# Head-major loads and quadrant transposes for part of q and k in a fused attention and feed-forward kernel

## The chip, the cores and the metric

The kernel runs on one core of one Trainium2 chip. The metric is the device time of one execution in microseconds (us), lower is better. A kernel is executed several times in alternation with the kernel before on the same chip; executions are marked fast or slow by time and by TensorE's granted clock, and only fast ones are compared. Profiles are of single executions; their span starts at the first instruction and is about 2 us shorter than the device time.

Names: PE is TensorE's matmul, PEld its weight load, DVE VectorE, ACT ScalarE, POOL GpSimd, SP SyncE. L907 is line 907 of the kernel whose profile is shown.

## The reference

Sliding-window causal attention with a linear bias, followed by a gated feed-forward over the 8 heads joined. B is 8, H 8, S 576, D 64, and everything comes and goes in float32.

```python
scores = q @ k.T / sqrt(D)                       # per batch and head
mask = (rel >= 0) & (rel < 128)                  # rel = query position - key position
scores = where(mask, scores - slope[h] * abs(rel), -1e9)
attn = softmax(scores)
x = (attn @ v) joined over heads                 # [8, 576, 512]
x_prev = x shifted by one position
xk = mu_k * x + (1 - mu_k) * x_prev              # xr in the same way
k = relu(xk @ w_k); v = (k * k) @ w_v            # 512 -> 1024 -> 512
out = sigmoid(xr @ w_r) * v
```

## The kernel before

The kernel is written as a graph of operations with durations and priorities. When it is built, a small simulator inside it (`plan`) picks, engine by engine, the ready operation of best priority, and the instructions are emitted in that order. So the order on each engine is fixed in the program, and every change of a load, a duration or a setting lets the simulator pick a new order for all engines.

Scores need q and k with the head dimension on the partitions. They are loaded with the positions on the partitions, cast to bf16 by the DMA, and transposed by PE against an identity. Two heads of 64 make one 128x128 transpose, so the two heads must lie side by side for a fixed row `r`, and each (position, head) is a run of its own: 64 float32, 256 bytes. The code is cut and shortened.

```python
def half_load(i, part, r, h0, h1):               # batch 0, second half (part 1)
    src = (q, k)[i][0, h0:h1, 256 * part:256 * part + 256].rearrange("h (p r) d -> p h r d", p=128)
    dst = half_buf[:, part, i, r, h0:h1]         # [p, part, i, r, h, d]: heads adjacent for one r
    return dma(POOL, ..., lambda e: nc.gpsimd.dma_start(out=dst, in_=src[:, :, r]))

def full_load(b, i, h, g):                       # a whole later batch: four DMAs, one per r
    src = (q, k)[i][b, :, 0:SM].rearrange("h (p r) d -> p h r d", p=128)   # (XB batches: cut)
    return [dma(POOL, ..., lambda e, r=r: nc.gpsimd.dma_start(
        out=cb_buf[h.idx][:, i, r], in_=src[:, :, r]), [g]) for r in range(NF)]

def qk_full(b, g, prio):                         # two heads: 8 transposes, 1 bank, 1 copy on ACT
    hp, hq = Hold(PT), Hold("qk")
    def emit_t(e):
        for n in range(2 * NF):
            nc.tensor.transpose(one(hp).bitcast(BF16)[:, 128 * n:128 * n + 128],
                cb_buf[hc.idx][:, n // NF, n % NF, 2 * g:2 * g + 2].rearrange("p h d -> p (h d)"), ident)
    t = op(PE, 0.0565 * 8, cl[b] + paced(b, g), prio + (3,), emit_t, [hp, hq], [hc])
    y = op(ACT, act_t(1024), [t], prio + (3,), lambda e: copy_any(e, ...), (), [hp])
# ... batch 0, part 1 does the same with half_buf and four transposes a pair of heads ...

LOADS = 'vK23tVkabcRWw'   # order of loads: K, k = halves of w_k, 2 = q and 3 = k of part 1,
                          # t = last 64 positions of batch 0, a b c = batch 1, R W w = other weights
MMASK = True              # the decay mask made by PE (mask_pe) and one exp; False: by ACT from dist
NWARM = 90                # matmuls of zeros, lowest priority: they fill PE where nothing is ready
for i in range(NWARM):
    plan.add(PE, 0.118 if i < 40 else 0.056, 0.0, [n_warm, g_wm], (1e12, i), emit_warm, (), [h_wm])
```

The softmax here doesn't subtract the row's maximum and nothing guards it: scores larger than these inputs give would overflow.

## Time and profile before

| | before |
|---|---|
| device time, three first runs | 237.60, 237.68, 238.79 us |
| span of the profiled run | 235.8 us, clock 1.00 |
| busy share PE / DVE / ACT / POOL | 96 / 80 / 68 / 43% |
| DMA packets under 512 bytes | 129,304 of 138,555 |

PE is the bound. The windows view gives, for each stretch, the busy time of PE, PEld, DVE, ACT and POOL with the number of instructions, then the granted clock, DMA share and GB/s. Kernel before:

```profile
core 0: us, PE busy (x) PEld busy (x) DVE busy (x) ACT busy (x) POOL busy (x), PEclk, DMA share, GB/s
20.00:25.00 5.00, 5.00 (x82) 3.13 (x81) 2.26 (x8) 4.46 (x10) 4.08 (x6) 1.00 2.27 162
25.00:30.00 5.00, 4.51 (x65) 3.61 (x62) 4.96 (x16) 4.08 (x10) 4.70 (x6) 1.00 2.41 151
```

Between 20 and 25 us PE counts as full while DVE is idle more than half of the time: a stage with room. Between 25 and 30 DVE is full and PE is not.

### The profile page before, as it was taken

The page shows a single profiled execution, that of the slowest core. Times are in us where ns is not written, and L with a number is a line of the kernel's source. Part 1 is how long each engine was busy: PE and PEld are TensorE (multiplying, and loading weights), DVE is VectorE, ACT ScalarE, POOL GpSimd, SP SyncE. Part 2 cuts the span into 40 slices and gives each one's busy share as a digit, 9 for nine tenths or more (in the row PEclk, how much of TensorE's full clock was granted, in tenths as well). Part 3 has the DMA queues.
Part 4 walks back from the last instruction along what each step waited for, and adds up shares of the span by engine and source line. Part 5 has one row for each costly group of instructions (what it writes and reads, how often), then busy time and mean ns, then how long its engine had stood idle before and what let it go on. Part 6 is the DMA issues. An engine that isn't in the chain of part 4 may idle for free.

```text
span 235.8 us, 5966 instructions
## 1 busy us (share of the span) xinstructions
PE 227.3 (96%) x2334; PEld 138.7 (59%) x2363; DVE 188.5 (80%) x425; ACT 160.5 (68%) x280; POOL 102.3 (43%) x128
## 2 busy tenths in 40 slices
PE   7999989999999999999999999999999999999993
PEld 7586776557575765555565765455665754445462
DVE  7393976999787999999998999974789995984242
ACT  3749799659988978984986684938475826326260
POOL 8878885697886595197109646100000000000000
PEclk9999999999999999999999999999999999999999
DMA  6999999999999999999999999995331224121112
GB/s 162 181 146 163 154 145 195 157 203 193 154 131 177 138 138 203 134 125 154 204 159 118 97 190 188 154 103 140 114 78 49 89 70 119 46 92 47 69 64 89
DMA packets 138555, 31.45 MB, mean 133 GB/s; under 512 B 129304, under 2 KB 134944, under 8 KB 138528
## 3 DMA queue, kind: packets, MB, share of 16 engines
q0 software_dynamic: 110992, 16.26, 109.5%
q1 hardware_dynamic: 25792, 14.23, 28.5%
q10 hardware_dynamic: 1744, 0.59, 1.0%
q8 instruction: 18, 0.29, 0.6%
q14 instruction: 9, 0.07, 0.1%
HBM read 33.56 MB, written 9.44 MB: 182 GB/s over the span
## 4 chain that ended last, share of the span: by engine, by line
PE 82%; ACT 7%; DMA 4%; issue 3%; POOL 3%; DVE 0%; DVEq 0%; POOLq 0%
PE uno L929 26%; PE uno L895 23%; PE uno L913 13%; PE duo L704 6%; PE duo L646 6%; DMA qx<-in_k_dram 4%; ACT rl L902 2%; PE uno L759 2%; ACT qk L616 2%; ACT at L660 2%; PE uno L1116 2%; POOL qx L430 1%; PE duo L633 1%; POOL vs L433 1%; PE uno L704 1%
## 5 line engine op out<-in xcount | busy, mean ns | idle before, releaser
L929 PE MATMUL uno<-wv_sb,kk 128*128 128x512 bf16 (+2 forms) x283 | 70.3, 373 | 0.9 <-issue 0.3
L895 PE MATMUL uno<-xk,wk_sb 128*128 128x256 bf16 (+2 forms) x412 | 69.4, 313 | 0.6 <-ACT qk L616 0.3
L660 ACT ACTIVATE at<-duo 128x1024 bf16<-128x1024 f32 (+2 forms) x68 | 65.9, 1008 | 2.7 <-PE duo L646 2.4
L902 ACT ACTIVATE rl<-uno 128x256 bf16<-128x256 f32 (+2 forms) x104 | 47.8, 506 | 19.5 <-PE uno L895 16.0
L895 PEld LDWEIGHTS <-wk_sb 128*128 128x128 bf16 x416 | 38.8, 98 | 22.1 <-issue 1.4
L868 DVE TENSOR_TENSOR kk<-rl 128x256 bf16<-128x256 bf16 (+2 forms) x104 | 33.6, 338 | 15.5 <-ACT rl L902 14.1
L929 PEld LDWEIGHTS <-kk 128*128 128x128 bf16 x296 | 26.5, 98 | 26.4
L433 POOL DMA_DIRECT2D vs<-in_v_dram x32 | 28.3, 897 | 28.2 <-PE duo L704 25.1
L920 ACT ACTIVATE rs<-uno 128x512 bf16<-128x512 f32 x36 | 22.1, 614 | 26.7 <-PE uno L913 24.3
L673 DVE TENSOR_TENSOR at<-at,mask 128x1024 bf16<-128x1024 bf16 x54 | 36.1, 684 | 3.5 <-ACT at L660 3.4
L913 PE MATMUL uno<-wr_sb,xr 128*128 128x512 bf16 x133 | 36.1, 379 | 0.5
L934 DVE SCALAR_TENSOR_TENSOR ot<-rs,uno 128x512 f32<-128x512 bf16 (+2 forms) x37 | 24.5, 667 | 14.5 <-PE uno L929 9.8
L455 POOL DMA_DIRECT2D cb<-in_k_dram x28 | 24.8, 902 | 11.6 <-DMA vs<-in_v_dram 4.9
L616 ACT COPY xt<-uno 128x320 bf16<-128x320 bf16 (+1 forms) x45 | 16.0, 404 | 15.2 <-PE uno L759 12.5
L455 POOL DMA_DIRECT2D cb<-in_q_dram x28 | 24.7, 906 | 2.5 <-DMA vs<-in_v_dram 1.0
L704 PEld LDWEIGHTS <-at 128*128 128x128 bf16 x576 | 21.9, 98 | 6.6 <-issue 1.1
L809 DVE SCALAR_TENSOR_TENSOR xk<-dl,mu_sb,xt 128x576 bf16<-128x576 bf16 (+1 forms) x32 | 24.9, 779 | 0.3
L809 DVE SCALAR_TENSOR_TENSOR xr<-dl,mu_sb,xt 128x576 bf16<-128x576 bf16 (+1 forms) x32 | 24.7, 776 | 0.0
L913 PEld LDWEIGHTS <-xr 128*128 128x128 bf16 x144 | 13.5, 98 | 14.6
L616 ACT COPY qk<-uno 128x1024 bf16<-128x1024 bf16 (+1 forms) x22 | 19.2, 929 | 2.3 <-PE uno L1014 1.9
L704 PE MATMUL duo<-vs,at 128*128 128x65 bf16 x448 | 19.1, 194 | 0.3 <-ACT at L660 0.2
L715 DVE TENSOR_TENSOR xu<-duo,rc 128x640 bf16<-128x640 f32 x20 | 16.4, 819 | 0.2
(73 smaller groups left out, 206.6 us busy)
## 6 DMA issues: line engine op xcount, KB each, us to landing
out_dram<-ot SPq DMA_DIRECT2D x28, 256.0 KB, 4.9
vs<-in_v_dram POOLq DMA_DIRECT2D x32, 128.0 KB, 6.5
cb<-in_q_dram POOLq DMA_DIRECT2D x28, 128.0 KB, 7.6
cb<-in_k_dram POOLq DMA_DIRECT2D x28, 128.0 KB, 7.0
out_dram<-ot SPq DMA_DIRECT2D x14, 128.0 KB, 1.8
wk_sb<-in_moe_w_k_dram POOLq DMA_DIRECT2D x2, 512.0 KB, 7.9
wv_sb<-in_moe_w_v_dram POOLq DMA_DIRECT2D x2, 512.0 KB, 10.7
qx<-in_k_dram ACTq DMA_DIRECT2D x4, 128.0 KB, 4.8
```

The lines of the kernel that those rows point to most:

```text
L433: return dma(POOL, 256, issue_t(1024), lambda e: nc.gpsimd.dma_start(out=vs_buf[h.idx][:, j, :, 0:D], in_=v[b, :, 128 * j:128 * j + 128].r ...
L455: return [dma(POOL, 256, issue_t(1024), lambda e, r=r: nc.gpsimd.dma_start(out=cb_buf[h.idx][:, i, r], in_=src[:, :, r]), [g]) for r in ra ...
L616: (nc.scalar.copy if e == ACT else nc.vector.tensor_copy)(out=out, in_=in_)
L660: lambda e, ah=ah, w=w, hp=hp: nc.scalar.activation(out=ah(), in_=two(hp)[:, :, 0:w], func=AF.Exp, scale=float(scale)), (), [hp])
L673: nc.vector.tensor_tensor(out=a, in0=a, in1=m, op=ALU.mult)
L704: nc.tensor.matmul(a[:, hl, t - t0], lhsT=at[:, lo:lo + 128], rhs=vs[:, u, 2 * g + hl, :] if u < NF else tvb[:, 2 * g + hl], start=(u == u ...
L809: lambda e: nc.vector.scalar_tensor_tensor(out=buf[hk.idx][:, g, e0 + c0:e0 + c1], in0=dls(), scalar=mu[:, g:g + 1], in1=xc(1), op0=ALU.mu ...
L868: nc.vector.tensor_tensor(out=out, in0=in_, in1=in_, op=ALU.mult)
L895: nc.tensor.matmul(one(hp)[:, 0:n], lhsT=wk_sb[:, po, 128 * fo:128 * fo + 128], rhs=xk_buf[hx.idx][:, po, c0:c1], start=(po == 0), stop=(p ...
L902: a = op(ACT, act_t(n), [s], pr, lambda e, hp=hp, hr=hr: nc.scalar.activation(out=rl_buf[hr.idx][:, 0:n], in_=one(hp)[:, 0:n], func=AF.Rel ...
L913: nc.tensor.matmul(one(hp), lhsT=xr_buf[hx.idx][:, po, 128 * c:128 * c + 128], rhs=wr_sb[:, po], start=(po == 0), stop=(po == NPO - 1))
L929: nc.tensor.matmul(one(hv)[:, a:b], lhsT=kk_buf[hk.idx][:, fo, o:o + 128], rhs=wv_sb[:, fo, a:b], start=(fo == 0), stop=(fo == NFO - 1))
```

## The change

The intent is to have the second half of batch 0's q and k earlier, and batch 1's cheaper, by longer runs. In head-major order a (position group, head) pair is one run of two rows (512 bytes) for batch 0 and four rows (1024 bytes) for batch 1. The price is the layout: for a fixed row the two heads are no longer side by side, so the kernel no longer takes both in one transpose. Each 128x128 block becomes four 64x64 transposes, one in each quadrant of the array; the two row halves write to two PSUM banks, and each bank has a copy of its own. The four part-1 loads also move ahead of the first half of w_k, and ten settings of the scheduler were tuned with the rest.

```diff
-    LOADS = 'vK23tVkabcRWw'
-    XD = 7
+    LOADS = 'v23KtVkabcRWw'
+    XD = 6
-    WAIT = 0.0
+    WAIT = 2.0                                   # price of a change between PE modes in the plan
-    XT0 = (ACT, DVE)
-    QK0 = (ACT,)
+    XT0 = (ACT,)
+    QK0 = (ACT, DVE)                             # who copies batch 0's q and k
-    XTT = range(8, B)
-    MMASK = True
+    XTT = range(6, B)                            # batches whose tails a DMA transposes
+    MMASK = False
-    A = {PE: 10.00, ACT: 3.00, DVE: 5.00, VIR: 0}
-    NBIAS = 5
-    XRL = 4.0
+    A = {PE: 14.25, ACT: 4.00, DVE: 4.50, VIR: 0}
+    NBIAS = 4                                    # groups whose bias PE adds
+    XRL = 3.0
-    SLOPE = 4.6
+    SLOPE = 4.5
-    def half_load(i, part, r, h0, h1):
...
+    def run_load(dst, i, b, c0, r, h0, h1, deps=()):
+        hs = (q, k)[i][b, h0:h1, c0:c0 + 128 * r].rearrange("h (p r) d -> p h (r d)", p=128)
+        return dma(POOL, RUN[r] * (h1 - h0), issue_t(128 * (h1 - h0)), lambda e: nc.gpsimd.dma_start(
+            out=dst()[:, i, h0:h1].rearrange("p h r d -> p h (r d)"), in_=hs), deps)
...
+    def qk_quad(b, g, nr, buf, deps, prio, c0, hq, take, free):
+        hp = [Hold("p1"), Hold("p1")]
+        def emit(e):
+            for n in range(2 * nr):
+                for hl, r in ((0, 0), (1, 1), (1, 0), (0, 1)):
+                    rows = slice(64 * r, 64 * r + 64)
+                    nc.tensor.transpose(
+                        one(hp[r]).bitcast(BF16)[64 * hl:64 * hl + 64, 64 * n:64 * n + 64],
+                        buf()[rows, n // nr, 2 * g + hl, n % nr], ident[rows, rows])
...  (two copies, one for each bank; batch 1 and part 1 of batch 0 call this; the rest as before)
```

More of the change, by code (lines that the diff above doesn't have):

```diff
@@ L220 @@
     RATE = 284.0
+    WIDE = (1,)
+    PART_WIDE = True
+    QUAD = 0.0565
+    RUN = {2: 64 * 284 / 329.0, NF: 128 * 284 / 357.0}
     FLIP = 1.25
     NO = 5
-    WAIT = 0.0
+    WAIT = 2.0
     QM = 0
@@ L262 @@
         "p (a i r h d) -> p a i r h d", a=2, i=2, r=2, d=D)
+    part_buf = qx_buf[0].rearrange("p i g s -> p (i g s)")[:, 2048:4096].rearrange(
+        "p (i h r d) -> p i h r d", i=2, r=2, d=D)
+    wide_buf = [c.rearrange("p i r h d -> p (i r h d)").rearrange(
+        "p (i h r d) -> p i h r d", i=2, r=NF, d=D) for c in cb_buf]
     stage = qx_buf[1].rearrange("p i g s -> p (i g s)").bitcast(FP32).rearrange(
@@ L422, in issue_t @@
         return 0.53 + 0.00034 * nd
-    def half_load(i, part, r, h0, h1):
-        src = (q, k)[i][0, h0:h1, 256 * part:256 * part + 256].rearrange(
-            "h (p r) d -> p h r d", p=128)
-        dst = half_buf[:, part, i, r, h0:h1]
-        nh = h1 - h0
-        return dma(POOL, 32 * nh, issue_t(128 * nh),
-                   lambda e: nc.gpsimd.dma_start(out=dst, in_=src[:, :, r]))
+    def run_load(dst, i, b, c0, r, h0, h1, deps=()):
+        hs = (q, k)[i][b, h0:h1, c0:c0 + 128 * r].rearrange("h (p r) d -> p h (r d)", p=128)
+        return dma(POOL, RUN[r] * (h1 - h0), issue_t(128 * (h1 - h0)), lambda e: nc.gpsimd.dma_start(
+            out=dst()[:, i, h0:h1].rearrange("p h r d -> p h (r d)"), in_=hs), deps)
     def v_load(b, j, h, deps=()):
@@ L450, in tail_load, with wide_load @@
         return h, ns
+    def wide_load(b, h, g, h0, h1):
+        return [run_load(lambda: wide_buf[h.idx], i, b, 0, NF, h0, h1, [g]) for i in range(2)]
     def full_load(b, i, h, g):
@@ L513 @@
     n_row = [mu_load(0, moe_mu_k), mu_load(1, moe_mu_r)]
-    th, tl, n_w, src1 = {}, {}, {}, []
+    th, tl, n_w, src1 = {}, {}, {}, {}
     vl[0] = []
@@ L529, in load_step @@
         elif what in "23":
-            src1.extend(half_load(int(what) - 2, 1, r, 0, 8) for r in range(2))
+            h0 = 4 * (int(what) - 2)
+            src1[h0 // 4] = [run_load(lambda: part_buf, i, 0, 256, 2, h0, h0 + 4) for i in range(2)]
         elif what == "t":
@@ L543, in load_step @@
             batch_load(1, what)
-    ch, cl, xbh, xbl, tth, ttl, ttg = {}, {}, {}, {}, {}, {}, {}
+    cw, ch, cl, xbh, xbl, tth, ttl, ttg = {}, {}, {}, {}, {}, {}, {}, {}
     def tail_flip(b):
@@ L559, in batch_load @@
             g_ = virtual("cb", [ch[b]])
-            cl[b] = full_load(b, 0, ch[b], g_) + full_load(b, 1, ch[b], g_)
+            if b not in WIDE:
+                cl[b] = full_load(b, 0, ch[b], g_) + full_load(b, 1, ch[b], g_)
+            else:
+                cw[b] = [wide_load(b, ch[b], g_, 4 * j, 4 * j + 4) for j in range(2)]
         elif what == "b":
@@ L980 @@
              (((3, 384, 128), (3, 512, 64), (4, 512, 64)), 512)))
+    def qk_quad(b, g, nr, buf, deps, prio, c0, hq, take, free):
[7 more added lines that the diff above has]
+                        buf()[rows, n // nr, 2 * g + hl, n % nr], ident[rows, rows])
+        t = op(PE, QUAD * 2 * nr, list(deps) + [n_ident], prio + (3,), emit,
+               hp + ([hq] if take else []), free)
+        t.rows, t.lazy = (64, 64), True
+        w = 64 * nr
+        ys = [op(QK0 if b == 0 else ACT, {ACT: act_t(2 * w), DVE: dve_t(2 * w)}, [t], prio + (3,),
+                 lambda e, r=r: copy_any(
+            e, qk_buf[hq.idx][:, :, c0 + w * r:c0 + w * r + w].rearrange("p t (c r) -> p t c r", r=nr),
+            one(hp[r]).bitcast(BF16)[:, 0:2 * w].rearrange("p (t r c) -> p t c r", t=2, r=nr)),
+                 (), [hp[r]]) for r in range(2)]
+        return hq, ys
     xks, xrs = {}, {}
@@ L1002 @@
             else:
-                cs = src1
-            hp = Hold("p1")
+                cs = src1[g // 2]
+            hp = Hold("p1") if part == 0 else None
             def emit_t(e, part=part, g=g, hp=hp, f32=f32):
@@ L1015, in emit_t @@
                             one(hp).bitcast(BF16)[:, 128 * nn:128 * nn + 128],
-                            half_buf[:, part, i, r, 2 * g:2 * g + 2].rearrange("p h d -> p (h d)"),
+                            half_buf[:, 0, i, r, 2 * g:2 * g + 2].rearrange("p h d -> p (h d)"),
                             ident)
-            cold = 1.8 if part == 0 and g < 2 else 1.0
-            t = op(PE, (0.115 if f32 else 0.0565) * 4 * cold, cs + [n_ident], prio + (3,), emit_t,
-                   [hp] + ([hq0[g]] if part == 0 else []))
-            y = op(QK0, {ACT: act_t(512), DVE: dve_t(512)}, [t], prio + (3,),
-                   lambda e, part=part, g=g, hp=hp, f32=f32: copy_any(
-                e, qk_buf[hq0[g].idx][:, :, 0:256],
-                one(hp).rearrange("p (t c) -> p t c", t=2)) if f32 else copy_any(
-                e, qk_buf[hq0[g].idx][:, :, 256 * part:256 * part + 256].rearrange(
-                    "p t (c r) -> p t c r", r=2),
-                one(hp).bitcast(BF16)[:, 0:512].rearrange("p (t r c) -> p t c r", t=2, r=2)),
-                (), [hp])
+            if part:
+                ys = qk_quad(0, g, 2, lambda: part_buf, cs, prio, 256, hq0[g], False, [])[1]
+            else:
+                cold = 1.8 if part == 0 and g < 2 else 1.0
+                t = op(PE, (0.115 if f32 else 0.0565) * 4 * cold, cs + [n_ident], prio + (3,), emit_t,
+                       [hp] + ([hq0[g]] if part == 0 else []))
+                ys = [op(QK0, {ACT: act_t(512), DVE: dve_t(512)}, [t], prio + (3,),
+                       lambda e, part=part, g=g, hp=hp, f32=f32: copy_any(
+                    e, qk_buf[hq0[g].idx][:, :, 0:256],
+                    one(hp).rearrange("p (t c) -> p t c", t=2)) if f32 else copy_any(
+                    e, qk_buf[hq0[g].idx][:, :, 256 * part:256 * part + 256].rearrange(
+                        "p t (c r) -> p t c r", r=2),
+                    one(hp).bitcast(BF16)[:, 0:512].rearrange("p (t r c) -> p t c r", t=2, r=2)),
+                    (), [hp])]
             ha = Hold("at")
@@ L1033 @@
                 s, (x,) = scores(0, g, [(pieces, m0, htt if uses_tt else None)], True, hq0[g], ha,
-                              [y, n_dist] + list(n_copy.values()) + n_sid[2 * g:2 * g + 2] +
+                              ys + [n_dist] + list(n_copy.values()) + n_sid[2 * g:2 * g + 2] +
                               (n_tt if uses_tt else []) + ([s] if j else []), prio,
@@ L1141 @@
                 pace = []
-                if not QM:
+                if b in WIDE:
+                    two_q[:] = [qk_quad(b, g, NF, lambda b=b: wide_buf[ch[b].idx], cw[b][g // 2] + paced(b, g),
+                                        prio, 0, Hold("qk"), True, [ch[b]])]
+                elif not QM:
                     two_q[:] = [qk_full(b, g, prio)]
@@ L1145 @@
                     two_q[:] = qk_some(b, g, QM, prio)
-                hq, y = two_q[g % max(QM, 1)]
+                hq, y = two_q[0 if b in WIDE else g % max(QM, 1)]
             _, (m0, m1) = scores(b, g, [HALF0 + (None,), HALF1 + (htt,)], 4 * b + g < NBIAS, hq, ha,
```

## The prediction

> **What bounds the kernel now.** I read the page's totals first, then the slices, then the chain that ended last and PE's timeline.
>
> ```profile
> PE 227.3 (96%) x2334; PEld 138.7 (59%) x2363; DVE 188.5 (80%) x425; ACT 160.5 (68%) x280; POOL 102.3 (43%) x128
> PE   7999989999999999999999999999999999999993
> PE 82%; ACT 7%; DMA 4%; issue 3%; POOL 3%; DVE 0%; DVEq 0%; POOLq 0%
> ```
>
> PE is busy 96% of the span and nearly full in every slice but the first and last. DVE (80%) and ACT (68%) are not the bound over the whole. So a change pays if it takes work off PE, or fills a gap of PE. But "busy" includes 90 warm matmuls (L607) that compute nothing. The chain and PE's timeline show where they stand:
>
> ```profile
> 2.26 1.87 POOL vs L433 x2
> 4.13 0.76 POOL wk_sb L465
> 4.88 2.58 POOL qx L430 x3
> 7.47 8.53 DMA qx<-in_k_dram
> 16.04 0.90 PE uno L1014 x13
> ...
> 30.39 1.25 ACT qk L616 x2
> ...
> 32.06 1.07 ACT qk L616
> ...
> 33.41 0.91 ACT qk L616
> ```
> ```profile
> 12.48 1.56 PE L607 MATMUL uno<-warm 128*128 128x128 bf16 x25
> ...
> 13.98 1.17 PE L607 MATMUL uno<-warm 128*128 128x128 bf16 x18
> ...
> 16.04 0.90 PE L1014 MATMUL uno<-ident,qx 128*128 128x128 bf16 x13 [0.38 <-DMA qx<-in_k_dram]
> ...
> 29.27 0.61 PE L1116 MATMUL uno<-ident,cb 128*128 128x128 bf16 x8
> ```
>
> The end hangs first on the issue of four loads, then on the landing of the second half of batch 0's k at 16.0; until then PE spins on warm matmuls. Around 30 to 34 us the chain runs through ACT's copies of batch 1's q and k out of PSUM; from 38 us it is almost only PE.
>
> **A ledger of PE.** I priced every PE instruction after 9.18 us (the first attention product with v) from the chain's rows: 512 columns 0.216 us (L929 x4, 0.86), 256 columns 0.109 (L895 x8, 0.87), 65 columns 0.030 (L704 x18, 0.55), a 128x128 transpose 0.056 (L1116 x16, 0.89), work on 64 rows half of that, as two run side by side. A change between 128-row and 64-row work costs about 0.08: in
>
> ```profile
> 45.84 0.86 PE uno L913 x4
> 46.70 0.55 PE duo L646 x12
> 47.25 0.97 PE uno L929 x4
> ```
>
> the twelve score matmuls are 8 x 0.055 + 4 x 0.015 = 0.50, and together the middle and last rows are 0.16 above price, for two changes. Walking the built program with these prices gives 215.7 us from 9.18 to the last matmul; the trace needs 222.7 (its last PE piece ends at 231.9). So 7 us are lost to waits and bubbles. Set against the timeline, 3.4 us of it is lost before 32.3 (0.6 at the first v, 0.7 around the landing at 16, 1.6 between 27 and 32 where xu on DVE and the qk copies on ACT are late), 1.7 up to 69 and some 2 in crumbs later. About 3.9 us of the span lie after the last matmul.
>
> **What the skill says.**
> - "TensorE: Matmul & The Clock Gate", Back-to-back issue gap: N/2.4 + 2.5 ns warm. The trace agrees (0.216 for 512).
> - "TensorEngine Tiling (Array Packing)", Key Properties: changing the tiling mode drains TensorE. The trace agrees (0.08 us each way). 64x64 mode has four independent tiles; the same page's Restrictions say that column tiling disables Fast Weight Load. No instruction before has column tiles, so no trace shows what a quadrant transpose costs.
> - "DMA: Bandwidth & Descriptors", Why small descriptors are slow: about 3 cycles of overhead per packet, 11 for 256 B. Then 512 B take 19 and 1024 B 35, 14% and 20% less per byte. The trace shows at least this (below).
>
> **The change, part by part.**
> *Loads.* Landing is issue plus issue-to-landing of each tile. Before: v 8.6 and 9.5, first wk half 11.8, q 12.8 and 13.7, k 14.9 and 16.0. So 256 KB of source in 256-byte runs take about 0.95 us, and wk, 1 MB in 2 KB runs, 2.3. Over 16 engines that is 15 ns a run of 256 B and 72 of 2 KB; on a straight line about 7 + 0.032 per byte: 23 ns for 512 B, 39 for 1024 B. The change puts the four part loads ahead of wk, and each becomes 512 runs of 512 B, 32 an engine: 0.73 us. Estimated landings: 10.2 and 11.0 (heads 0 to 3), 11.7 and 12.4 (4 to 7), wk at 14.7. Issuing fits: four at some 0.7 us from 4.1 end near 6.9. Batch 1's q and k fall from 8 x 0.95 = 7.6 to 4 x 32 x 39 ns = 5.0, so all of them are there near 25 instead of 29.
> *PE, head.* In the new order, PE's first quadrant transposes stand right after the part-0 scores, at 10.8 by the ledger; with the 0.6 lost at v they meet data that landed at 11. The wait at 16 goes. But the 90 warm matmuls stay: only their places change (77 instead of 90 before the tail transposes), so all 3.0 us of warm work after 9.18 are still paid. The four to five us that the early landing seems to offer are thus not there; what can be had is idle time: 0.7 at the landing, and perhaps 0.9 of the later waits, since evacuations start earlier and are less bunched.
> *PE, work.* Gone: 8 mask matmuls of 256 (0.87 us), 4 bias matmuls of 512 of batch 1's first group (0.86), 8 tail transposes of batches 6 and 7 that become DMA transposes (0.45): 2.18. Replaced: 48 transposes of 128x128 (2.7 us) by 192 of 64x64. At 14 ns each, two side by side, that is again 2.7. Mode changes rise from 96 to 106: +0.83. Net 2.18 - 0.83 = 1.35 less.
> *ACT and DVE.* ACT makes the mask itself: 8 x about 0.37 (estimated from 0.43 for a 256-wide pass, less the overlap) for two of 1.05, +0.9. Batch 1's copies become eight of about 0.6 for four of 1.05, +0.6. DVE gets two more mask products (2 x 0.68), a share of batch 0's copies, and loses two tail copies (2 x 0.41), about +1.5. Both lie in stages where ACT was half idle (10 to 20 us: 5.96 of 10 busy) or where DVE follows PE; I charge nothing beyond halving the hoped recovery. The later retuning of priorities I put at 0 +/- 0.7.
> *Sum.* 1.35 (work) + 0.7 (landing) + 0.9 (other waits) = 3.0 us, at quadrants of 14 ns. I weigh the dearer quadrant below at 0.6 us, which leaves 2.4: 237.7 - 2.4 = 235.3.
>
> **Rivals.**
> 1. *Quadrants are weight-load bound.* Each transposed block is itself the stationary operand, and without the fast load 64 columns may take as long as a lone 64-column matmul, 29 ns, with no overlap. Then 192 x 0.029 = 5.6 us instead of 2.7, PE gains 2.9, and the change is worth nothing: 238. For it: 192 weight loads for 48, and the page's restriction. Against: the row-tiled transposes of L759 run ten in 0.25 us including a mode change. I give it one in five.
> 2. *Four run fully side by side*, 7 ns each: 1.4 us less than priced, 233.5. One in six.
> 3. *ACT takes the place of the load.* ACT was full from 30 to 40 us (two windows of 5.00 of 5.00), and gets 1.5 us more before that. If it stays the limit there, PE waits for qk and rl as before, the 0.9 and part of the 0.7 vanish: 236.8. One in four.
> 4. *The early landing counts in full*: the batch 0 chain shifts by 4 to 5 us and so does the end, 233 or below. Against it stands the ledger: the order is fixed and the warm matmuls are in it. One in eight.
>
> **Range and chances.** Rivals 1 and 3 put the upper side at 238, 2 and 4 the lower at 232.7. Faster by over 2% means under 232.9: it needs 2 or 4, and no new wait, 0.14. Slower by over 2% (above 242.4) would take a long new wait that nothing in the order suggests, 0.02. Within 2%: 0.84.
>
> **What would show it.** Right: the DMA piece to 16.0 is gone from the chain and quadrant transposes start near 11 us; 16 of them take about 0.25 us and 32 about 0.45; warm matmuls still number 90 and about 13 run after 16 us; the last matmul ends near 229.5; PE busy falls by two to three us. Wrong: 32 quadrants in 0.9 us or more (rival 1) or 0.25 (rival 2); PE waits on ACT's qk or rl totalling over 1.5 us between 20 and 40 (rival 3); waits on the first wk half or on the tails, moved behind; or gaps after 60 us that the new priorities bring.

## The result, and the profile after

The changed kernel took 234.94, 235.29, 235.53 and 235.66 us, a median of 235.41, beside 237.60 to 238.79 and a median of 237.90 for the kernel before on the same chip. The ratio is 0.9887, with a 95% interval of 0.9855 to 0.9919. Here and below a ratio is the mean time of one kernel's fast runs over the mean of the kernel before's fast runs of the same rounds, so it is not quite the ratio of the medians quoted. The change is real, about 1.1%, and within the 2% that counts as the same.

The page of the kernel after: the totals, PE in 40 slices, and the chain's shares by engine.

```profile
PE 225.8 (97%) x2487; PEld 135.7 (58%) x2487; DVE 189.8 (81%) x427; ACT 160.8 (69%) x292; POOL 97.7 (42%) x124
...
PE   7899989999999999999999999999999999999994
...
PE 84%; ACT 5%; DMA 3%; POOL 3%; issue 2%; DVE 1%; DVEq 0%; POOLq 0%; ACTq 0%
```

PE does more instructions in less time, and more of the chain is PE. POOL has fewer issues (124 for 128). The span fell from 235.8 to 233.1.

The chain of waits of the kernel after (start, us, what):

```profile
7.87 0.70 POOL ts L453
8.60 8.04 DMA ts<-in_k_dram
16.69 0.40 PE uno L856 x4
...
18.08 1.30 ACT at L672 x2
...
28.44 0.47 PE uno L1002 x32
28.91 0.58 ACT qk L628
...
227.23 2.18 PE uno L941 x12
```

The landing of part 1's k at 16.0 is gone, yet a DMA still ends at 16.6: the last 64 positions of batch 0 (`ts`), which were issued in the same place as before (8.6 for 9.0 us) and are needed by the same scores. Before, they landed at about 17.4 (8.4 us after their issue), so that what holds the second half of batch 0 moved by some 0.75 us and not by four or five. And the last matmuls end at 229.41, where those of before ended at 231.81.

PE's timeline of the kernel after (start, us, then what; in brackets the idle time before it and what ended it):

```profile
10.96 0.32 PE L1002 MATMUL uno<-ident,qx 64*64 64x64 bf16 x16
11.21 0.22 PE L609 MATMUL uno<-id,mu_row 8*128 8x8 f32 x1
...
15.81 0.83 PE L619 MATMUL uno<-warm 128*128 128x128 bf16 x12
16.69 0.40 PE L856 MATMUL uno<-ident,ts 128*128 128x128 bf16 x4
...
28.37 0.99 PE L1002 MATMUL uno<-ident,cb 64*64 64x64 bf16 x64
29.53 0.27 PE L856 MATMUL uno<-ident,ts 128*128 128x128 bf16 x2 [0.17 <-ACT qk L628]
30.29 0.27 PE L856 MATMUL uno<-ident,ts 128*128 128x128 bf16 x2 [0.49 <-issue]
```

Sixteen quadrant transposes at 10.96 are followed by the next instruction 0.25 us later. That is not 16 ns each: in the trace's single records four of them start within 10 ns, one in each quadrant, and the next four follow 32 ns later (the first time 42), so a row costs 8 ns a transpose, and about 0.12 us go by from the last start to the next instruction, which is of another mode. At 15.81 twelve warm matmuls stand where PE has nothing else to do until `ts` is there. At 30.29, right after 64 quadrants, PE stands half a microsecond for nothing that the profile shows ("issue").

The window of the stage with room, kernel after:

```profile
20.00:25.00 5.00, 5.00 (x98) 3.97 (x92) 3.79 (x12) 5.00 (x14) 2.88 (x4) 1.00 1.53 192
```

Before, ACT was busy 4.46 us of these five and DVE 2.26; now ACT is full and DVE at 3.79, and the DMA share fell from 2.27 to 1.53. The room in this stage was used.

**The ledger.** The prediction priced every PE instruction and compared the sum with the timeline. The same was done for each kernel below, with 0.083 us for a mode change; *loss* is the timeline less the ledger, that is, waits and bubbles. Start is the first attention product with v. The prediction and the expectations price a quadrant at 14 ns (14.1 in the ledger). The records give 8.1, which makes 192 of them 1.15 us cheaper, so here and in the next table a quadrant is priced at 8.1 ns; the ledgers in the expectations are higher by 1.15 us (2.3 in quad_twice).

| | start | priced work | mode changes in it | loss by about 41 us | loss at the end |
|---|---|---|---|---|---|
| before | 9.18 | 215.7 | 92 | 3.8 | 7.2 |
| after, quadrants at 14.1 ns | 9.13 | 214.4 | 102 | 3.4 | 6.1 |
| after, quadrants at 8.1 ns | 9.13 | 213.3 | 102 | 4.5 | 7.2 |

So by the measured price the 2.4 us are 2.4 of work, and the loss is 7.2 in both, good to some tenths. About 2.1 of the work are the settings; the transposes save 1.1 (192 at 8.1 ns for 48 at 56 ns), and ten more mode changes take 0.8 of it back. Of the loss, after is 0.4 ahead at 20 us (1.0 for 1.42), some 0.3 behind at 30 and 0.7 behind at 41 and 52, and makes that up later, most of it between 53 and 65 us (0.5 lost there for 1.0). The early landing is therefore visible up to 20 us, more than that is given back by 41 us, and a stage with none of the changed loads in it makes up for it.

### The profile page after: what moved, and what is told of

It reads as the page before. It is cut to its first block, busy times and chain, and to the rows that moved or that the text cites. A ratio compares the mean times of both kernels' runs of the same rounds, so it can differ in the third digit from the quotient of the medians.

```text
span 233.1 us, 6268 instructions
## 1 busy us (share of the span) xinstructions
PE 225.8 (97%) x2487; PEld 135.7 (58%) x2487; DVE 189.8 (81%) x427; ACT 160.8 (69%) x292; POOL 97.7 (42%) x124
## 4 chain that ended last, share of the span: by engine, by line
PE 84%; ACT 5%; DMA 3%; POOL 3%; issue 2%; DVE 1%; DVEq 0%; POOLq 0%; ACTq 0%
PE uno L941 27%; PE uno L907 26%; PE uno L925 14%; PE duo L716 6%; PE duo L658 5%; DMA ts<-in_k_dram 3%; PE uno L771 2%; PE uno L1154 2%; ACT at L672 2%; POOL qx L434 1%; ACT mask L1088 1%; ACT qk L628 1%; PE uno L856 1%; POOL vs L438 1%; ACT rl L914 1%
## 5 line engine op out<-in xcount | busy, mean ns | idle before, releaser
L941 PE MATMUL uno<-wv_sb,kk 128*128 128x512 bf16 (+2 forms) x296 | 71.8, 374 | 0.0
L914 ACT ACTIVATE rl<-uno 128x256 bf16<-128x256 f32 (+2 forms) x104 | 47.3, 492 | 20.3 <-PE uno L907 19.0
L685 DVE TENSOR_TENSOR at<-at,mask 128x1024 bf16<-128x1024 bf16 x56 | 37.7, 680 | 8.2 <-ACT at L672 7.8
L880 DVE TENSOR_TENSOR kk<-rl 128x256 bf16<-128x256 bf16 (+2 forms) x104 | 32.8, 334 | 9.0 <-ACT rl L914 7.8
L925 PE MATMUL uno<-wr_sb,xr 128*128 128x512 bf16 x144 | 37.0, 379 | 0.5 <-ACT rl L914 0.5
L463 POOL DMA_DIRECT2D cb<-in_k_dram x24 | 21.3, 901 | 7.1 <-DMA wv_sb<-in_moe_w_v_dram 3.3
L628 ACT COPY xt<-uno 128x256 bf16<-128x256 bf16 (+1 forms) x48 | 17.1, 405 | 9.0 <-PE uno L771 8.8
L463 POOL DMA_DIRECT2D cb<-in_q_dram x24 | 21.2, 915 | 1.4 <-DMA vs<-in_v_dram 1.2
L628 ACT COPY qk<-uno 128x1024 bf16<-128x1024 bf16 (+2 forms) x26 | 18.8, 777 | 2.4 <-PE uno L1049 0.8
L814 DVE TENSOR_TENSOR dl<-xt 128x576 bf16<-128x576 bf16 (+1 forms) x32 | 13.7, 434 | 4.2 <-ACT xt L628 4.2
```

The lines of the kernel that those rows point to most:

```text
L463: return [dma(POOL, 256, issue_t(1024), lambda e, r=r: nc.gpsimd.dma_start(out=cb_buf[h.idx][:, i, r], in_=src[:, :, r]), [g]) for r in ra ...
L628: (nc.scalar.copy if e == ACT else nc.vector.tensor_copy)(out=out, in_=in_)
L685: nc.vector.tensor_tensor(out=a, in0=a, in1=m, op=ALU.mult)
L880: nc.vector.tensor_tensor(out=out, in0=in_, in1=in_, op=ALU.mult)
L914: a = op(ACT, act_t(n), [s], pr, lambda e, hp=hp, hr=hr: nc.scalar.activation(out=rl_buf[hr.idx][:, 0:n], in_=one(hp)[:, 0:n], func=AF.Rel ...
L925: nc.tensor.matmul(one(hp), lhsT=xr_buf[hx.idx][:, po, 128 * c:128 * c + 128], rhs=wr_sb[:, po], start=(po == 0), stop=(po == NPO - 1))
```

## The experiments

Theory: the gain is the sum of two independent terms, less PE work by the settings and less waiting by the earlier landing. Rivals: the halves only work together, since they shift a fixed order; the gain sits in the order alone; or the quadrants or the warm matmuls hold more time than they show. Twelve kernels were run, all of them correct, on three chips. All are compared with the kernel before.

| run | what | median us | before there | ratio (95%) | work | loss |
|---|---|---|---|---|---|---|
| tune_only | before + settings | 238.45 | 238.50 | 1.0000 (0.9956 to 1.0043) | 213.6 | 10.2 |
| tune_order | same + load order | 238.10 | 238.50 | 0.9994 (0.9952 to 1.0036) | 213.9 | 8.6 |
| runs_only | after, settings and order of before | 238.24 | 238.50 | 0.9994 (0.9957 to 1.0031) | 215.2 | 8.0 |
| runs_order | after, settings of before | 239.53 | 238.50 | 1.0051 (1.0015 to 1.0087) | 215.7 | 8.7 |
| order_back | after, load order of before | 238.86 | 237.65 | 1.0064 (1.0021 to 1.0106) | 213.6 | 9.4 |
| pe_mask | after, mask on PE | 240.74 | 237.65 | 1.0124 (1.0097 to 1.0151) | 214.3 | 11.9 |
| warm60 | after, 60 warm matmuls | 245.25 (243.66 of the fast runs) | 237.65 | 1.0261 (1.0207 to 1.0315) | 211.6 | 16.2 |
| quad_twice | after, each quadrant twice | 244.40 | 237.65 | 1.0282 (1.0238 to 1.0326) | 214.8 | 15.4 |
| short_runs | after, runs cut to 256 bytes | 243.38 | 238.03 | 1.0210 (1.0164 to 1.0256) | 213.3 | 15.1 |
| old_loads | the same, first w_k half ahead | 243.44 | 238.03 | 1.0205 (1.0158 to 1.0252) | 213.3 | 16.7 |
| warm_skip | after, 53 warm matmuls left out | 236.63 | 238.03 | 0.9922 (0.9880 to 0.9965) | 210.3 | 11.0 |
| col_tiles | after, two column tiles a block | 241.85 | 238.03 | 1.0156 (1.0109 to 1.0203) | 214.2 | 13.0 |

In the first seven the plan is made anew, so the whole order may shift. In the next four (quad_twice, short_runs, old_loads, warm_skip) the traces show the order of the kernel after on PE, ACT and DVE, apart from the edit. col_tiles was meant to keep it too, but did not: in its trace DVE has another order from 13 us on and ACT from 17 us on, so it belongs with the first seven.

Of the twelve expectations only those of tune_only and runs_only hold a range that the time fell into. The other ten kernels came out slower than every range set for them. One reason that nobody had priced is the clock: in the traces of warm60, quad_twice, short_runs and warm_skip it is granted at half for 3.4 us before the end, in old_loads for 3.4 and again for 6.8, each time after stretches in which PE had stood waiting. Work at half clock takes twice as long, so 3.4 us cost up to 1.7 (an estimate), which the table counts as loss.

### The halves of the change

tune_only and tune_order are the kernel before with the settings of after, and the second also with the load order:

```diff
-    LOADS = 'vK23tVkabcRWw'
+    LOADS = 'v23KtVkabcRWw'      # tune_order only
+    XD = 6; WAIT = 2.0; XT0 = (ACT,); QK0 = (ACT, DVE); XTT = range(6, B); MMASK = False
+    A = {PE: 14.25, ACT: 4.00, DVE: 4.50, VIR: 0}; NBIAS = 4; XRL = 3.0; SLOPE = 4.5
```

> The old loads in the old order, with only the new settings (mask on ACT, four bias groups, tails by DMA, priorities). The PE ledger after the first product with v is 213.6 us (before 215.7, after 214.4). Theory 1, PE's work sets the time: with the 6.1 to 7.2 us of losses that the two traces show, 234.9 to 236.0 us, most of the gain of 2.5 us without any longer run. Theory 2, the early landing is what gained: the wait for k at 16 us stays and the time is within 0.7 us of the 237.9 of before.

> As tune_only, and the second-half loads of batch 0 ahead of the first wk half, still in 256-byte runs and with 128x128 transposes. Ledger 213.9 us. Theory 1: 235.0 to 235.9 us, at most 0.7 us from tune_only. Theory 2: the move ahead brings the landing from 16 to about 13.7, so half or more of the 2.5 us appears here and not in tune_only.

runs_only and runs_order are the kernel after with the settings of before, and the first also with its load order:

```diff
-    LOADS = 'v23KtVkabcRWw'
+    LOADS = 'vK23tVkabcRWw'      # runs_only only
+    XD = 7; WAIT = 0.0; XT0 = (ACT, DVE); QK0 = (ACT,); XTT = range(8, B); MMASK = True
+    A = {PE: 10.00, ACT: 3.00, DVE: 5.00, VIR: 0}; NBIAS = 5; XRL = 4.0; SLOPE = 4.6
```

> The long runs and quadrant transposes in the old order of loads and with all settings of before. Ledger 216.3 us, 0.5 more than before through six more mode changes. Theory 1: 237.2 to 238.5 us, no gain. Theory 2: batch 1 is there 3 us earlier and batch 0's second half 1 us earlier, so 236.5 us or less.

> Long runs and quadrants, and batch 0's second half ahead of wk, with all other settings of before. Ledger 216.8 us, 1.0 more than before; the wait of 0.7 us at the landing goes. Theory 1: 237.7 to 238.8 us. Theory 2: the landing near 11.5 us instead of 16 is all here, so 235.4 to 236.2 us, as after.

Measured: 1.0000, 0.9994, 0.9994 and 1.0051. No half gains anything that these rounds can see, and loads with the new order but the old settings lose a little. The work column is prices times counts, so it confirms no price by itself. By it the settings take 2.1 us away (213.6 for 215.7, predicted 2.18), and the loads with their quadrants 0.5 (215.2). But with the settings alone the loss rises by 3.0 us and eats the work saved, and with the loads alone by 0.8. PE's waits of tune_only between 9 and 80 us (us in total, times, longest) say where:

```profile
PE uno L742 <- DVE xu L715: 1.1, 1, 1.1
PE uno L1014 <- DMA qx<-in_k_dram: 1.0, 1, 1.0
PE duo L646 <- ACT at L660: 0.8, 2, 0.5
```

Part 1's k lands as late as ever, and now PE waits 1.0 us for it where it was 0.4. That is only 0.6 of the 3.0 us: tune_order's list of waits has no wait for k, and its loss is still 8.6. So the sum of two independent terms falls: in these plans work taken off PE came back as waits, with the late loads and with the earlier ones, and early loads under the old settings gained nothing. Together the two are worth 1.1%. What in the new plan makes them go together, these runs don't show.

### Single steps undone, with a new plan

order_back takes the load order back, pe_mask puts the mask on PE again, and warm60 has fewer warm matmuls:

```diff
-    LOADS = 'v23KtVkabcRWw'
+    LOADS = 'vK23tVkabcRWw'      # order_back
-    MMASK = False
+    MMASK = True                 # pe_mask
-    NWARM = 90
+    NWARM = 60                   # warm60
```

> The changed kernel with the first wk half ahead of batch 0's second-half q and k again; runs, quadrants and settings as changed. Ledger 214.7 us (changed kernel 214.4). If the early landing is what lets the lighter PE work count, the landing goes back by some 2.3 us to near 14, the loss by 42 us rises from 3.4 to 4.5 or more and the ratio to before is 0.993 to 0.998. If the order of loads does not matter, 0.988 to 0.990.

> The changed kernel with the mask made by PE and two ACT passes again. Ledger 215.4 us, 1.0 more. If PE's work sets the time also in the head, the ratio to before rises from 0.989 to 0.993. If the head is held by ACT (5.00 of 5.00 busy from 20 to 25 us), PE has room there and ACT is relieved by about 0.9 us, so the ratio stays at 0.986 to 0.990.

> The changed kernel with 60 warm matmuls instead of 90. Ledger 212.7 us, 1.7 less. If the warm matmuls in the head stand in the way of real work, as the prediction held, the time falls by 1.7 us, ratio 0.982. If they only fill waits, PE waits instead: the loss rises by what the work falls, and the ratio stays at 0.988 to 0.990.

Measured: 1.0064, 1.0124 and 1.0261 (two of warm60's six runs were slow and are left out of the ratio). Against the kernel after that is 4, 6 and 9 us, if the ratios of two chips may be set against each other by 0.9887. The priced work changed by +0.3, +1.0 and -1.7 us and the first product with v came 0.2 to 0.6 us later; the rest is loss, +2.2, +4.7 and +9.0. The largest waits of PE between 9 and 80 us, order_back:

```profile
PE uno L907 <- DVE xk L821: 1.5, 1, 1.5
```

pe_mask:

```profile
PE duo L658 <- ACT at L672: 1.9, 3, 1.1
```

warm60:

```profile
PE duo L658 <- ACT at L672: 2.7, 3, 1.2
PE uno L907 <- ACT qk L628: 2.4, 2, 1.3
```

None of these is a wait for the thing that was edited. The rise of order_back's loss by 42 us that was expected did not come; its one large wait ends at 57.6 us. pe_mask loses 2.2 us between 55 and 60 us, far from the masks (the kernel after loses under 0.5 there), and 30 warm matmuls of 56 ns (1.7 us) cannot be 9 us. What changed is the order as a whole. These three don't price the mask, the load order or the warm matmuls. They show that the kernel after sits in a narrow spot: each of these three new plans around it cost 2 to 9 us of waits.

### Quadrants doubled

```diff
-                for hl, r in ((0, 0), (1, 1), (1, 0), (0, 1)):
+                for hl, r in ((0, 0), (1, 1), (1, 0), (0, 1)) * 2:
```

> The changed kernel with each quadrant transpose done twice, same order, right result. Ledger 217.1 us, 2.7 more at 14 ns a transpose. If PE's work sets the time in the head, 2.7 us more, ratio 1.000. If the head is held by ACT and the loads, much of it falls in waits: 0.5 to 1.5 us more, ratio 0.991 to 0.995.

Measured: 244.40 us, a ratio of 1.0282. PE's timeline of quad_twice:

```profile
10.99 0.45 PE L1002 MATMUL uno<-ident,qx 64*64 64x64 bf16 x32
11.36 0.22 PE L609 MATMUL uno<-id,mu_row 8*128 8x8 f32 x1
...
26.77 0.66 PE L1002 MATMUL uno<-ident,cb 64*64 64x64 bf16 x58
29.51 0.25 PE L1002 MATMUL uno<-ident,cb 64*64 64x64 bf16 x6 [2.08 <-issue]
...
32.49 1.08 PE L1002 MATMUL uno<-ident,cb 64*64 64x64 bf16 x99
36.53 0.63 PE L1002 MATMUL uno<-ident,cb 64*64 64x64 bf16 x29 [2.96 <-issue]
```

The first two lines give the price. Here 32 transposes start at 10.99 and the next instruction at 11.36; in the kernel after it was 16 at 10.96 and the next at 11.21. Sixteen more take 0.13 us, 8 ns each, and so they do in the other three rows of batch 0. That is four side by side and not two: the 192 extra transposes are 1.6 us, not 2.7. (With 14.1 ns the ledger finds no loss at all up to 20 us, where the kernel after, in the same order, has 0.6: the price was too high.) Then 11 us are lost between 20 and 44 us, where the kernel after loses 3.5.

PE stops in the middle of a row of transposes that all have their data, and its waits on "issue" up to 44 us sum to 8.0 us. From the restart at 29.51 to the next stop the timeline has 6 + 12 + 3 + 8 + 99 = 128 matmuls; with their weight loads that is 256 instructions. From 36.53 to the stop at 41.9 it has 127. The DMA view has a queue of its own for instructions: between 26.5 and 29.6 us it moved one packet.

```profile
q8 instruction: 1, 0.02, 2.3%
```

The records of that queue are packets of 16 KB, 21 in the run. Four of them moved at 20.61 to 21.56, 26.87 to 28.03, 33.94 to 34.87 and 41.40 to 42.38 us, and PE restarted at 23.04, 29.51, 36.53 and 43.64, always 1.3 to 1.7 us after the packet's end. The Trainium skill, "Runtime: NRT & Kernel Launch", section "Instruction fetch mechanics", says that instructions come in blocks of 16 KiB, 256 instructions, and that crossing into the next is mostly hidden. The trace agrees on the block, and shows it not hidden here: 128 quadrants and their weight loads take about 1.0 us, and the next block is not there yet. The number of packets fits the instructions of PE: the matmuls and weight loads of before, after and quad_twice are 18.5, 19.4 and 20.9 times 256, and the queue moved 18, 19 and 21 packets. The kernel after has this stop once: a packet from 27.21 to 28.42, a restart at 30.29 after 0.49 us of "issue". No run varied the fetch alone, so this is read from the coincidence of five stops, 128 matmuls between two, and one packet at each; it was not tested by itself.

### The loads back, order kept

short_runs keeps everything and cuts each run into its rows; old_loads also puts the first half of w_k ahead of the part-1 loads again.

```diff
-        return dma(POOL, RUN[r] * (h1 - h0), issue_t(128 * (h1 - h0)), lambda e: nc.gpsimd.dma_start(...
+        def emit(e):
+            for rr in range(r):
+                nc.gpsimd.dma_start(out=dst()[:, i, h0:h1, rr], in_=hr[:, :, rr])
+        return dma(POOL, RUN[r] * (h1 - h0), issue_t(128 * (h1 - h0)), emit, deps)
...  # old_loads only, on the finished order:
+        moved = order.pop(wk0)
+        order.insert(at[0], moved)
```

> The changed kernel, same order of everything, with only the runs cut to 256 bytes (batch 0's second half still ahead of wk). Estimated landings 11.4 and 13.3 us for the two pairs instead of 10.3 and 11.9, batch 1 about 2.5 us later. If run length matters by itself: 0.5 to 2 us more, ratio 0.991 to 0.997. If only the order of loads matters: 0.987 to 0.990.

> The changed kernel with its instructions in exactly the same order on PE, ACT and DVE, and quadrants kept; only the loads go back: 256-byte runs, the first wk half ahead of batch 0's second half. If the early landing is what makes the new order pay, PE stands waiting from about 11 to 14 us and again near 26, and the time rises by 3 to 4.5 us, ratio 1.001 to 1.008. If the loads were hidden anyway, ratio 0.987 to 0.991.

Measured: 243.38 and 243.44 us, ratios of 1.0210 and 1.0205. Against the kernel after both are some 8 us slower, with the same priced work. PE's waits between 9 and 80 us, short_runs:

```profile
PE uno L930 <- DMA wr_sb<-in_moe_w_r_dram: 2.9, 1, 2.9
PE uno L1007 <- DMA cb<-in_k_dram: 2.9, 2, 1.9
```

old_loads:

```profile
PE uno L1010 <- DMA cb<-in_k_dram: 1.5, 3, 0.7
PE uno L1010 <- DMA qx<-in_q_dram: 1.4, 2, 1.1
```

So the new order needs the loads that it was made for. One confound must be named: cutting the runs also raises the number of DMAs, from 4 to 8 for batch 0 and from 4 to 16 for batch 1, each issued in about 0.74 us on POOL (busy 109.5 us for 97.7). In short_runs that pushes the issue of w_r and w_v to 36.4 us and later, and the 2.9 us wait for w_r is its consequence. The two runs show what short runs and their issues cost together, about 8 us in this order, the half clock included (old_loads: 0.66 from 15 to 20 us, 0.56 from 35 to 40); they don't show the run length alone, and the kernel before needed fewer issues for the same bytes (8 for batch 1, of 0.9 us). The landings in the traces say a little: where loads of batch 1 queue, 128 KB in 256-byte runs land every 0.43 us in short_runs, and 512 KB in 1024-byte runs every 1.3 us in the kernel after, a quarter less for each byte.

### Warm matmuls left out

The plan is made with 90, but those from the 38th on are not emitted; 53 fall away after the first product with v.

```diff
         plan.add(PE, 0.118 if i < 40 else 0.056, 0.0, [n_warm, g_wm], (1e12, i),
-                 emit_warm, (), [h_wm])
+                 emit_warm if i < 37 else None, (), [h_wm])
```

> The changed kernel, same order of everything, with the 53 warm matmuls after the first product with v left out (3.0 us of the ledger). If they stand in the way of real work, as the prediction said, the last matmul comes 1.5 to 3 us earlier, ratio 0.976 to 0.983. If they only fill waits for ACT, DVE and loads, the loss rises by nearly what the work falls: 0.986 to 0.990, or more should the granted clock fall.

Measured: 236.63 us, 0.9922, beside 0.9887 for the kernel after on another chip, their intervals overlapping. Taking 3.0 us of matmuls off PE gave no gain. The priced work fell to 210.3 and the loss rose to 11.0. The first wait of warm_skip, and its window from 15 to 20 us:

```profile
PE uno L857 <- DMA ts<-in_k_dram: 1.0, 1, 1.0
```
```profile
15.00:20.00 5.00, 3.97 (x59) 1.81 (x59) 4.33 (x12) 2.95 (x7) 3.52 (x5) 0.72 1.99 167
```

Where the warm matmuls had stood, PE now waits for `ts`, and its clock falls to 0.72 in this window (1.00 in the kernel after). The transposes of `ts` start at 16.93 us without the warm matmuls and at 16.69 with them, so the 40 that stood before `ts` were no cost: they stand inside a wait that is there anyway. And it names the wait: the next load in line. What the 13 later ones cost, the run can't say, since the clock changed too: the one execution of six with a granted clock of 1.00 took 234.94 us, the five others (0.98 to 0.99) 236.29 to 237.27.

### Two column tiles instead of four quadrants

Each block becomes two transposes of 128 rows by 64 columns into one bank, and both copies read that bank.

```diff
-                for hl, r in ((0, 0), (1, 1), (1, 0), (0, 1)):
-                    rows = slice(64 * r, 64 * r + 64)
+                for hl in range(2):
                     nc.tensor.transpose(
-                        one(hp[r]).bitcast(BF16)[64 * hl:64 * hl + 64, 64 * n:64 * n + 64],
-                        buf()[rows, n // nr, 2 * g + hl, n % nr], ident[rows, rows])
+                        one(hp[0]).bitcast(BF16)[64 * hl:64 * hl + 64, 128 * n:128 * n + 128],
+                        buf()[:, n // nr, 2 * g + hl, n % nr], ident)
```

> The changed kernel, same order, each group's transposes done in two column tiles of 128 rows by 64 columns into one bank: 96 transposes of 128 columns instead of 192 of 64, half the PE instructions; the two copies now read one bank. If two column tiles run side by side: 28 ns each, the same 2.7 us, six to ten mode changes stay, and the 0.5 us of issue after 64 quadrants goes: 0 to 0.8 us less, ratio 0.985 to 0.989. If they run one after another, 56 ns each: 2.7 us more, ratio 0.996 to 1.001.

Measured: 241.85 us, 1.0156. It halves the transposes (96 for 192) and still loses. In the records two start together every 56 ns, 28 ns each, so a 128x128 block takes 56 ns, as it does whole, and 32 in quadrants; the price in the table is 28 ns. By 41 us its loss is about 6, the kernel after's 4.5; most of the difference arises between 53 and 77 us, where nothing was edited, and the largest wait there is again ACT's:

```profile
PE duo L658 <- ACT at L672: 2.1, 4, 0.9
```

But ACT and DVE work in another order here (above), probably because the one bank is held until the second copy. So this run is one more new plan: quadrants are cheaper than column tiles by their records, 1.6 us for 2.7 in all, but what the exchange alone does to the time it doesn't show.

## Why the prediction was right

The time was predicted at 235.3 us, within 232.7 to 238.0, and most likely within 2%; it is 235.41. The number is right, but two errors behind it cancel: PE's work fell by more than was predicted, and its waits did not fall. Point by point:

- **The bound.** Right. PE stays full, and what counts is PE's work and PE's waits together.
- **PE work, 1.35 less.** Too small: it is 2.4 by the measured prices. The settings' part (2.18 predicted, 2.1) and the ten more mode changes (102 for 92) are as counted; the transposes, put at no change, save 1.1. PE busy fell by 1.5 us where 2 to 3 were expected; the records of before lack 29 matmuls (2334 for 2363 weight loads), so this row was not a fair test.
- **Quadrants at 14 ns.** Wrong: 8 ns, four side by side, in the kernel after and doubled. This is rival 2, put at 7 ns and one in six; rival 1 (29 ns) falls, and the 0.6 us held back for it was not needed. The sign that was set misled at first: 16 of them and the way out take 0.25 us, as said, but that is half fixed cost. 32 take 0.38 (from 32.35 us on), where 0.45 was to speak for 14 ns and 0.25 for rival 2. Not foreseen was a cost of their *number*: the stop for instructions, 0.5 us in the kernel after and 8.0 with the quadrants doubled.
- **Landing.** The part-1 loads landed 5.6 us after issue, so from 9.7 to 12.0 us; estimated 10.2 to 12.4. Transposes started at 10.96, as predicted. Of the 0.7 us hoped for at the landing 0.4 came by 20 us. Batch 1's last load landed at 27.0, not near 25.
- **Other waits up to 32 us, 0.9.** Wrong. By 41 us the kernel after has lost 0.7 more than the one before. ACT was full from 20 to 25 us and, with the stop for instructions, took back what was won; that is rival 3's outcome, though the waits that name ACT between 20 and 40 us sum to 1.1 us, under the 1.5 set as its sign. What was won back after 53 us the prediction had put at 0 +/- 0.7 for the retuning.
- **The sum.** Predicted: 1.35 + 0.7 + 0.9 - 0.6 = 2.4. By the ledger: 2.4 of work and about 0 of waits. That these agree is luck. Rival 2's price came with rival 3's waits.
- **The warm matmuls are "still paid".** Wrong for the 40 before `ts`; left out in the same order they return nothing (0.9922 for 0.9887). That rival 4 (the early landing in full) would not come was right, but for another cause: the tails of batch 0, issued where they were, land at 16.6 and hold the same scores. The prediction named waits on the tails as a sign of being wrong; the wait moved there and cost PE nothing more only because the warm matmuls stood in it.
- **Terms added up.** The prediction treats work and waits as separate terms. The runs of the halves speak against this: neither half alone moves the time (1.0000 and 0.9994), because waits take its place.

What stays open: how much of each loss in the runs with a new plan is the edited part and how much the new order; what run length alone does to the time; why the new plan with the new loads has no more waits than the old one, when each half alone has; and whether loading the tails ahead of the first half of w_k would free the stretch before 16.6. The last was not run. No run here beat the changed kernel.

## What to carry to other kernels

In a kernel whose order is fixed by a plan, work taken off the bound engine and a transfer made earlier need not be separate gains: run each half alone before crediting it, and look at which load comes next in line behind the one made faster. To test one part there, keep the order as it is and change that part alone; a new plan moves more than most parts are worth. Price a short instruction from two rows of different length: one row hides the fixed cost of its ends in the price. When many short matmuls replace a few long ones, count instructions as well as their time, and look for "issue" in PE's waits.

## What the Trainium skill lacked or had wrong

- "Runtime: NRT & Kernel Launch", Instruction fetch mechanics: it calls the cost of crossing a 16 KiB block mostly hidden. With rows of 64x64 transposes it was not: 0.5 us in the kernel after and 8.0 us in four stops with the quadrants doubled, each with one 16 KB packet whose end came 1.3 to 1.9 us before PE went on.
- "TensorEngine Tiling (Array Packing)", Key Properties: it says that a change of mode drains TensorE and gives no time. The traces fit 0.08 to 0.1 us for each change.
- The same section: tiles are said to work independently, and no time for transposes in 64x64 mode is given. The runs agree and give the time: four start within 10 ns, the next four 32 ns later, 8 ns for each of a row.
- "TensorE: Matmul & The Clock Gate", LDWEIGHTS: the time is said to follow the columns. The records of 64x64 weight loads are 107 to 108 ns long, those of 128x128 98, so in these records half the columns were no shorter; in a row they still come 8 ns apart on average.
- "DMA: Bandwidth & Descriptors", Why small descriptors are slow: it counts cycles per packet and gives no time for a run of a casting load. In the kernel before 256 KB of float32 in 256-byte runs landed every 0.95 us or so, but each was also issued in 0.91 us. Where loads queue behind one another, a 256-byte run took 13 ns on each of 16 engines (0.43 us for 512 runs, short_runs) and a 1024-byte run 41 ns (1.3 us for 512 runs, the kernel after).
